# Sliding-window attention with a gated FFN: key tiles that repeat the last keys of the tile before, in batches 2 and 3

## The chip, the cores and the metric

The kernel runs on one core of a Trainium2 chip. The metric is the device time of one execution in microseconds (us); lower is better. Three runs of the kernel before took 254.18, 252.22 and 251.6 us, a median of 252.22 us.

A core has five engines with instruction queues of their own. TensorE (PE) multiplies matrices and loads the stationary operand of each product (PEld). VectorE (DVE), ScalarE (ACT) and GpSimd (POOL) work elementwise. SyncE (SP) only issues DMA transfers here. Each engine [...]waits on semaphores for what others produce. Sixteen DMA engines move the data.

## The reference

```python
# q, k, v: (4, 8, 768, 64) float32; n_sink = 4, window = 128
scores = (q @ k.transpose(0, 1, 3, 2)) / sqrt(64)
rel = pos[:, None] - pos[None, :]
keep = (pos[None, :] < 4) | ((rel >= 0) & (rel < 128))
a = softmax(where(keep, scores, -1e9))
x = (a @ v).transpose(0, 2, 1, 3).reshape(3072, 512)
out = (maximum(x @ w_gate, 0) * (x @ w_val)) @ w_out   # w_gate, w_val: 512 x 1536; w_out: 1536 x 512
```

Each query sees the four first keys (the sinks) and the 128 keys that end with itself. The output of attention goes, token by token, through a gated feed-forward network (FFN) with a ReLU on the gate.

## The kernel before

**Units.** A unit is a pair of heads of one batch: four units per batch, sixteen in all, so units 8 to 11 are batch 2 and units 12 to 15 batch 3. Its two heads lie on partitions 0 to 63 and 64 to 127 of `KQ`, which holds the transposed queries in its first 768 columns and the keys (`kE`) behind them, 768 columns in order and 408 more for "odd" key tiles. Four `KQ` buffers go round.

**Key tiles.** A key tile has 128 rows. Seven tiles cover the 768 keys. The even ones (0, 2, 4, 6) are plain slices of the keys; the odd ones (1, 3, 5) consist of the four sinks and 124 keys, and are copied together on GpSimd by `odd_tiles` and `sinks` (L185, L181). The table `SEG` lists, per group of tiles, which key tile is multiplied with which queries and where in the score tile it lands: groups 0, 1 and 2 have 3, 3 and 4 segments per head. In each group one segment of three columns serves the last three queries that a query tile still needs from a key tile two places back. `QSEG` says, per query tile, which key tiles it adds up: 16 matmuls per head. The values lie in `vn` by the same tiles, with a column of ones behind each head, so that the 65th output column is the sum of the weights.

**Steps of a unit.** `Sg(u, s)` computes the scores of one group for both heads on TensorE (L290), takes exp on ScalarE (L298) and multiplies by a 0/1 mask (`msk`) on VectorE (L300). `W(u)` multiplies these weights with the values on TensorE (L325, stationary operand `ee`, 65 columns) and divides by the sum on VectorE into `xn` (L331). In batches 0 and 1 TensorE transposes queries, keys and `xn`. In batches 2 and 3 DMA does: `load_rows` brings queries and keys (`qf`, `kf`), `cast_rows` makes them bf16 on GpSimd (`qn`, `kn`, L166), `to_dram` writes them to a scratch tensor, and `turn` reads them back transposed into `KQ` (L175). `x_to_dram` writes `xn` to the scratch tensor `xd` (L151) and `x_turn` reads it back transposed into `xT` (L155). `load_v` brings one value tile of all eight heads (L131) and `cast_v` casts it on GpSimd (L134). All these transfers are issued by SP.

**The order.** It is written out by hand. The FFN's first half is cut into 96 chunks, 24 per batch; the loop goes through these slots. A chunk (`chunk`) is eight matmuls of up to 396 columns (L362), a ReLU on ScalarE (L377) and a product on VectorE (L379). From slot 24 on each slot adds three matmuls of the FFN's second half (L404). The attention of the next batch is put between them by the table `plan`: batch 2's scores start in slot 29 and its `W`s stand in slots 35, 37, 39 and 41; batch 3's scores start in slot 48 and its `W`s stand in slots 56, 58, 61 and 63. Batch 2's chunks begin in slot 48. The table `prep` puts GpSimd's work and the transfers in front of a slot's chunk: batch 2's value loads in slots 23 to 29 and casts in 28 to 34, batch 3's loads in 44 to 50 and casts in 47 to 53. Two rows of it matter most:

```python
            prep[at["S", i, 0] - 1].append(("sinks", i))
            prep[at["W", i, 0] + 1].append(("xd", i))
            prep[at["W", i, 0] + 3].append(("xturn", i))
        for b, s0, s1 in ((2, 23, 28), (3, 44, 47)):
            for j in range(7):
                prep[s0 + j].append(("lv", b, j))
                prep[s1 + j].append(("v", b, j))
```

Within a slot the entries are issued in the order in which they were appended. In slots 33 and 34 GpSimd's list is therefore: the casts of unit 12's keys and queries, value tile 5 of batch 2, the odd key tiles of unit 10, value tile 6.

Each transfer from SP counts up one of eight semaphores in turn, and waits where needed for the transfer that used it before, eight places back.

Of the kernel before, what the change touches and what calls it, by code (L numbers as in the profile page):

```python
# [10 lines left out]
BF16 = mybir.dt.bfloat16  # L11
Alu = mybir.AluOpType
# [9 lines left out]
def kernel(  # L22
# [12 lines left out]
    nc = tc.nc  # L35
    B, H, S, D = q.shape
    assert (B, H, S, D) == (4, 8, 768, 64)
    NP = H // 2
# [7 lines left out]
    const = ctx.enter_context(tc.tile_pool(name="const", bufs=1))  # L46
# [4 lines left out]
    NQ, NE, NT = 3, 4, 4  # L51
# [5 lines left out]
    KQ = [const.tile([128, 2 * S + 408], BF16, name=f"KQ{i}") for i in range(NT)]  # L57
    qT = [x[:, 0:S] for x in KQ]
    kE = [x[:, S:2 * S + 408] for x in KQ]
# [8 lines left out]
    xT = [const.tile([128, NP, S], BF16, name=f"xT{i}") for i in range(2)]  # L68
# [2 lines left out]
    warm = const.tile([128, 2], F32, name="warm")  # L71
    idle = const.tile([128, 512], BF16, name="idle")
    msk = const.tile([128, 3, 512], BF16, name="msk")
    mb = const.tile([128, 2, 512], BF16, name="mb")
    band = const.tile([128, 256], BF16, name="band")

# [5 lines left out]
    ODD = S  # L82
# [11 lines left out]
    QSEG = [[(0, 0, 0)], [(0, 0, 128), (1, 0, 252)], [(1, 0, 376), (2, 1, 0), (0, 0, 504)],  # L94
            [(2, 1, 128), (3, 1, 252)], [(3, 1, 376), (4, 2, 0), (2, 1, 504)],
            [(4, 2, 128), (5, 2, 272)], [(5, 2, 396), (6, 2, 252), (4, 2, 416)]]

    PART = {0: (range(3), 0, CUT0), 1: (range(3, 7), CUT0, S), None: (range(7), 0, S)}

# [4 lines left out]
    U = [Unit(i) for i in range(B * NP)]  # L104
# [17 lines left out]
    VROW = [0, 116, 244, 368, 496, 620, 748]  # L122

    def load_v(b, j, r0=0, r1=128):
        r1 = min(r1, S - VROW[j])

        parts = [(0, 4, 0), (4, 16, VROW[j] + 4), (16, 128, VROW[j] + 16)] if j in (1, 3, 5) else [(0, 128, VROW[j])]
        for a0, a1, s0 in parts:
            a1 = min(a1, r1)
            if r0 <= a0 < a1:  # L130
                nc.sync.dma_start(out=vf[a0:a1, j, :, :], in_=v[b, :, s0:s0 + a1 - a0, :].rearrange("h s d -> s h d"))  # L131
# [10 lines left out]
    kqd = [nc.dram_tensor(f"kqd{i}", (2 * S, 128), BF16, kind="Internal").ap() for i in range(ND, B * NP)]  # L142


    xd = [nc.dram_tensor(f"xd{i}", (1008, 128), BF16, kind="Internal").ap() for i in range(ND, B * NP)]

    def x_to_dram(u):

        x, d = xn[u.i % 2], xd[u.i - ND]
        for t, r0, n, i in ((0, 0, 128, 4), (1, 128, 124, 3)):  # L150
            nc.sync.dma_start(out=d[r0:r0 + 252 * i, :].rearrange("(i r) c -> r i c", r=252)[0:n, :, :],  # L151
                              in_=x[0:n, t:t + 2 * i - 1:2, :])

    def x_turn(u):
        nc.sync.dma_start(out=xT[u.b % 2][:, u.p, :], in_=xd[u.i - ND][8:8 + S, :], transpose=True)  # L155
        for x in range(2):
            ready[u.b, u.p, x] = True

# [20 lines left out]
    def sinks(u, copy):  # L179
        e = kE[u.i % NT]  # L180
        copy(odd(e)[:, :, 0:4], e[:, 0:4].unsqueeze(1).to_broadcast([128, 3, 4]))  # L181

    def odd_tiles(u, copy):
        e = kE[u.i % NT]
        copy(odd(e)[:, :, 4:128], e[:, 120:876].rearrange("d (i c) -> d i c", c=252)[:, :, 0:124])  # L185
        sinks(u, copy)

    def load_w(m0, m1, which=(0, 1)):
        for w, dst in (((moe_w_gate, wg), (moe_w_val, wv))[x] for x in which):
# [37 lines left out]
    def setup2(g):  # L227
# [6 lines left out]
        if g == 2:  # L234
            cp(msk[:, 2, 252:272], band[:, 0:20])

    rot = [0]

    def pair():
# [38 lines left out]

    def Sg(u, s, ps=None):
        t, bias = u.i % NT, u.b == 0 and s in (0, 3)  # L280
        g, b0, n, segs = SEG[s]
        ps = ps or pair()
        at = [ps[h][:] if isinstance(ps, list) else ps[:, h, :] for h in range(2)]
        if bias:
            for h in range(2):
                nc.tensor.matmul(out=at[h][:, b0:n], lhsT=ident[:], rhs=mb[:, g, b0:n], start=True, stop=False,
                                 skip_group_check=True)
        for x0, q0, c0, c1 in segs:
            for h in range(2):
                nc.tensor.matmul(out=at[h][:, c0:c1], lhsT=kE[t][64 * h:64 * h + 64, x0:x0 + 128],  # L290
                                 rhs=qT[t][64 * h:64 * h + 64, q0:q0 + c1 - c0], start=not bias, stop=True,
                                 skip_group_check=True)
        x = ee[u.i % NE][:, g, :, b0:n]
        if isinstance(ps, list):
            for h in range(2):
                nc.scalar.activation(x[:, h, :], at[h][:, b0:n], Act.Exp, bias=0.0, scale=scale)
        else:
            nc.scalar.activation(x, ps[:, :, b0:n], Act.Exp, bias=0.0, scale=scale)  # L298
        if not bias:
            nc.vector.tensor_tensor(x, x, msk[:, g, b0:n].unsqueeze(1).to_broadcast([128, 2, n - b0]), op=Alu.mult)  # L300

    ready = {}

# [5 lines left out]

    def W(u, part=None, bank=None):  # L310

        tiles = PART[part][0]
        n, w = len(tiles), 65 * len(tiles)
        if bank is None:
            ps = pair()
            at = [ps[:, 0, 0:w], ps[:, 1, 0:w]]
            o = ps[:, :, 0:w].rearrange("p h (t e) -> p h t e", e=65)
        else:
            at = [bank[:, 0:w], bank[:, w:2 * w]]
            o = bank[:, 0:2 * w].rearrange("p (h t e) -> p h t e", h=2, e=65)  # L320
        for h in range(2):
            for t in tiles:
                c = 65 * (t - tiles[0])
                for i, (j, g, c0) in enumerate(QSEG[t]):
                    nc.tensor.matmul(out=at[h][:, c:c + 65], lhsT=ee[u.i % NE][:, g, h, c0:c0 + 128],  # L325
                                     rhs=vn[u.b % 2][:, j, 2 * u.p + h, 0:65],
                                     start=c == 0 and i == 0 and (bank is None or h == 0),
                                     stop=t == tiles[-1] and i == len(QSEG[t]) - 1, skip_group_check=True)
# [82 lines left out]
    with tc.manual_schedule():  # L411
# [91 lines left out]
        for i, ts in ((8, (17, 20, 21, 24)), (9, (18, 21, 22, 26)), (10, (20, 23, 24, 28)), (11, (22, 24, 26, 30)),  # L503
                      (12, (30, 33, 35, 38)), (13, (32, 35, 37, 40)), (14, (34, 37, 39, 43)), (15, (36, 39, 41, 45))):
            for t, what in zip(ts, ("rows", "castrows", "td", "turn")):
                prep[t].append((what, i))
            assert at["S", i - NP, 2] < ts[3] < at["S", i, 0] - 1, i
            prep[at["S", i, 0] - 1].append(("sinks", i))
            prep[at["W", i, 0] + 1].append(("xd", i))
            prep[at["W", i, 0] + 3].append(("xturn", i))  # L510

        for b, s0, s1 in ((2, 23, 28), (3, 44, 47)):
            for j in range(7):
# [5 lines left out]
        for s, (b, g, m) in enumerate(slots):  # L519
            for x in prep[s]:  # L520
                if x[0] == "kq":
                    cast_rows(U[x[1]])
                elif x[0] == "load":
                    load_rows(U[x[1]])
                elif x[0] == "half":
                    cast_half(x[1])
                elif x[0] == "w":
                    load_w(*x[1:])
                elif x[0] == "wo":
                    for c in range(3):  # L530
                        load_wo(c)
                elif x[0] == "rows":
                    if x[1] in (8, 9):
                        gate(U[x[1]])
                    load_rows(U[x[1]])
                elif x[0] == "castrows":
                    cast_rows(U[x[1]])
                elif x[0] == "td":
                    to_dram(U[x[1]])
                elif x[0] == "setup3":  # L540
                    setup3()
                elif x[0] == "xd":
# [72 lines left out]
```

## Time and profile before

| quantity | value |
|---|---|
| median of three runs | 252.22 us |
| the profiled execution | 252.45 us |
| its span in the trace | 250.4 us |
| TensorE busy | 238.6 us, 95% |
| VectorE, ScalarE busy | 116.6 and 120.6 us |
| GpSimd busy | 69.7 us, 28% |
| DMA packets | 75681, of them 53512 under 512 bytes; 40.07 MB |

The profile's page gives the busy time of each engine, then the span in 40 slices of 6.26 us, each digit a busy share in tenths, and then the chain of work that ended last: from the last instruction back to whatever released it, step by step. Groups of instructions follow, with line, engine, operation, tiles, shapes, count, busy time, the mean duration of one in ns, and the idle time ahead of them with what ended it. The busy time of overlapping matmuls is counted once, so their means are longer than their distance in time. In the timelines and in the chain each row has its start and its duration in us; "SPq" is SP's queue, whose rows are issues of transfers, and "DMA" in the chain is the time until one has landed.

### The profile page before, as it was taken

The page shows a single profiled execution, that of the slowest core. Times are in us where ns is not written, and L with a number is a line of the kernel's source. Part 1 is how long each engine was busy: PE and PEld are TensorE (multiplying, and loading weights), DVE is VectorE, ACT ScalarE, POOL GpSimd, SP SyncE. Part 2 cuts the span into 40 slices and gives each one's busy share as a digit, 9 for nine tenths or more (in the row PEclk, how much of TensorE's full clock was granted, in tenths as well). Part 3 has the DMA queues.
Part 4 walks back from the last instruction along what each step waited for, and adds up shares of the span by engine and source line. Part 5 has one row for each costly group of instructions (what it writes and reads, how often), then busy time and mean ns, then how long its engine had stood idle before and what let it go on. Part 6 is the DMA issues. An engine that isn't in the chain of part 4 may idle for free.

```text
span 250.4 us, 5321 instructions
## 1 busy us (share of the span) xinstructions
PE 238.6 (95%) x2084; PEld 139.9 (56%) x2084; DVE 116.6 (47%) x224; ACT 120.6 (48%) x220; POOL 69.7 (28%) x125
## 2 busy tenths in 40 slices
PE   7879969999999999999999999999999999999994
PEld 2456556655775555666555556565555555555443
DVE  5565854688662354687325546544322232222000
ACT  4849926999253455552336664532333323333111
POOL 7856664982633225631003600000000000000000
PEclk9999999999999999999999999999999999999999
DMA  6999999999989999899899311443211011110232
GB/s 207 251 211 259 245 338 235 213 164 219 337 274 231 242 184 323 278 230 210 211 227 229 82 42 39 106 106 77 75 44 42 0 42 46 43 42 1 86 126 84
DMA packets 75681, 40.07 MB, mean 160 GB/s; under 512 B 53512, under 2 KB 72712, under 8 KB 75656
## 3 DMA queue, kind: packets, MB, share of 16 engines
q1 hardware_dynamic: 67560, 34.10, 52.6%
q0 software_dynamic: 6864, 4.72, 12.7%
q10 hardware_dynamic: 1232, 0.92, 1.1%
q8 instruction: 16, 0.26, 0.4%
q14 instruction: 9, 0.07, 0.1%
HBM read 28.48 MB, written 11.25 MB: 159 GB/s over the span
## 4 chain that ended last, share of the span: by engine, by line
PE 70%; DMA 15%; SPq 6%; POOL 4%; issue 2%; ACT 1%; DVE 0%; POOLq 0%; DVEq 0%; ACTq 0%
PE g L362 38%; PE g L404 20%; SPq L131 5%; PE pp L325 4%; DMA vf<-in_v_dram 4%; DMA kf<-in_k_dram 4%; DMA wv<-in_moe_w_val_dram 3%; PE pp L404 3%; DMA qf<-in_q_dram 3%; PE pp L290 2%; POOL vn L134 1%; POOL ee L308 1%; SPq L113 1%; PE pp L398 1%; PE g L398 1%
## 5 line engine op out<-in xcount | busy, mean ns | idle before, releaser
L379 DVE TENSOR_TENSOR hT<-gs,g 128x384 bf16<-128x384 f32 (+2 forms) x96 | 53.0, 553 | 88.3 <-PE g L362 80.2
L377 ACT ACTIVATE gs<-g 128x384 f32<-128x384 f32 (+2 forms) x96 | 47.7, 497 | 77.0 <-PE g L362 75.9
L362 PE MATMUL g<-xT,wv 128*128 128x384 bf16 (+2 forms) x384 | 78.8, 326 | 2.7 <-DMA wv<-in_moe_w_val_dram 2.6
L362 PE MATMUL g<-xT,wg 128*128 128x384 bf16 (+2 forms) x384 | 78.8, 326 | 0.5 <-ACT xT L345 0.5
L404 PE MATMUL g<-wo,hT 128*128 128x512 bf16 x240 | 64.0, 379 | 0.3 <-ACT ot L408 0.2
L362 PEld LDWEIGHTS <-wv 128*128 128x128 bf16 x384 | 37.3, 98 | 29.1 <-DMA wv<-in_moe_w_val_dram 3.8
L362 PEld LDWEIGHTS <-wg 128*128 128x128 bf16 x384 | 36.2, 98 | 30.3
L298 ACT ACTIVATE ee<-pp 128x838 bf16<-128x838 f32 (+4 forms) x50 | 43.0, 904 | 9.5 <-PE pp L290 9.2
L404 PEld LDWEIGHTS <-hT 128*128 128x128 bf16 x276 | 25.5, 98 | 23.8 <-issue 0.7
L300 DVE TENSOR_TENSOR ee<-ee,msk 128x838 bf16<-128x838 bf16 (+3 forms) x44 | 32.2, 738 | 13.8 <-ACT ee L298 13.2
L134 POOL CAST vn<-vf 128x512 bf16<-128x512 f32 x27 | 18.6, 706 | 33.7 <-DMA vf<-in_v_dram 33.7
L325 PEld LDWEIGHTS <-ee 128*128 128x128 bf16 x512 | 18.1, 97 | 5.1 <-issue 3.2
L408 ACT COPY ot<-g 128x512 f32<-128x512 f32 x20 | 11.7, 587 | 17.5 <-PE g L404 17.5
L325 PE MATMUL pp<-vn,ee 128*128 128x65 bf16 x488 | 18.2, 193 | 1.4 <-POOL vn L134 1.3
L331 DVE TENSOR_TENSOR xn<-pp,rn 128x896 bf16<-128x896 f32 (+2 forms) x18 | 17.0, 943 | 0.6
L290 PEld LDWEIGHTS <-KQ 64*128 64x128 bf16 x328 | 10.9, 94 | 10.1 <-issue 8.2
L290 PE MATMUL pp<-KQ 64*128 64x3 bf16 (+5 forms) x316 | 15.8, 221 | 0.0
L166 POOL CAST kn<-kf 128x768 bf16<-128x768 f32 x12 | 10.2, 851 | 17.2 <-DMA kf<-in_k_dram 8.9
L166 POOL CAST qn<-qf 128x768 bf16<-128x768 f32 x12 | 11.3, 940 | 2.8 <-DMA qf<-in_q_dram 2.5
L185 POOL COPY KQ<-KQ 128x372 bf16<-128x372 bf16 x12 | 6.3, 529 | 11.5 <-DMA KQ<-kqd 6.8
L345 ACT COPY xT<-g 128x372 bf16<-128x372 bf16 (+2 forms) x10 | 5.4, 545 | 6.8 <-PE g L342 6.8
L404 PE MATMUL pp<-wo,hT 128*128 128x512 bf16 x36 | 8.1, 379 | 0.0
(80 smaller groups left out, 105.5 us busy)
## 6 DMA issues: line engine op xcount, KB each, us to landing
out_dram<-ot SPq DMA_DIRECT2D x23, 256.0 KB
kf<-in_k_dram SPq DMA_DIRECT2D x12, 384.0 KB
qf<-in_q_dram SPq DMA_DIRECT2D x12, 384.0 KB
vf<-in_v_dram SPq DMA_DIRECT2D x12, 256.0 KB
vf<-in_v_dram SPq DMA_DIRECT2D x12, 224.0 KB
kf<-in_k_dram SPq DMA_DIRECT2D x8, 192.0 KB
wo<-in_moe_w_out_dram POOLq DMA_DIRECT2D x3, 512.0 KB, 8.6
kqd<-qn SPq DMA_DIRECT2D x8, 192.0 KB
```

The costliest lines, as they stand in the source:

```text
L131: nc.sync.dma_start(out=vf[a0:a1, j, :, :], in_=v[b, :, s0:s0 + a1 - a0, :].rearrange("h s d -> s h d"))
L134: copy(vn[b % 2][0:rows, j, :, 0:64], vf[0:rows, j, :, :])
L166: nc.gpsimd.tensor_copy(dst[u.i % 2][:].rearrange("p (n h d) -> p h n d", n=NR, h=2), src[u.i % NQ][:].rearrange("p (h n d) -> p h n d", n ...
L290: nc.tensor.matmul(out=at[h][:, c0:c1], lhsT=kE[t][64 * h:64 * h + 64, x0:x0 + 128], rhs=qT[t][64 * h:64 * h + 64, q0:q0 + c1 - c0], start ...
L298: nc.scalar.activation(x, ps[:, :, b0:n], Act.Exp, bias=0.0, scale=scale)
L300: nc.vector.tensor_tensor(x, x, msk[:, g, b0:n].unsqueeze(1).to_broadcast([128, 2, n - b0]), op=Alu.mult)
L325: nc.tensor.matmul(out=at[h][:, c:c + 65], lhsT=ee[u.i % NE][:, g, h, c0:c0 + 128], rhs=vn[u.b % 2][:, j, 2 * u.p + h, 0:65], start=c == 0 ...
L331: nc.vector.tensor_tensor(x.rearrange("p t (h d) -> p h t d", h=2), o[:, :, :, 0:64], r.unsqueeze(3).to_broadcast([128, 2, n, 64]), op=Alu ...
L362: nc.tensor.matmul(out=ps[:, 0:n], lhsT=w[:, ko, m * 128:(m + 1) * 128], rhs=x[:, ko, c], start=ko == 0, stop=ko == KO - 1)
L377: nc.scalar.activation(gs[:, 0:n], gp[:, 0:n], Act.Relu, bias=0.0, scale=1.0)
L379: nc.vector.tensor_tensor(h[:, m, c], gs[:, 0:n], vp[:, 0:n], op=Alu.mult)
L404: nc.tensor.matmul(out=op, lhsT=hT[b % 2][:, m, t * 128:(t + 1) * 128], rhs=wo[:, m, :], start=m == 0, stop=m == FM - 1)
```

## The change

In batches 2 and 3 the key tiles are cut anew, at keys 0, 128, 256, 380, 504, 625, 746 and 768 (`K2`). From tile 2 on a tile begins with repeated rows (`LEAD`): the four sinks (tiles 2, 4, 6), and the last 3 or 6 keys ahead of the tile before it (tiles 3 and 4, tiles 5 and 6). A query tile then needs its own key tile and the one before it, and nothing else. Groups 0, 1 and 2 have 2, 2 and 3 segments per head (`SEG2`), `QSEG2` has 13 matmuls per head, and a second mask (`msk2`) is built by `setup4` on GpSimd in slots 25 to 27. `key_tiles` takes the place of `odd_tiles` and puts tiles 2 to 6 together behind the keys in `KQ`, which grows by 232 columns. `load_v` loads each value tile in the same order of rows, in up to four transfers, and `x_to_dram` stores the seven query tiles without overlap in four transfers. Batches 0 and 1 stay as they are.

```diff
+    K2 = [0, 128, 256, 380, 504, 625, 746, S]
+    LEAD = [(0, 0), (0, 0), (4, 0), (0, 3), (4, 3), (0, 6), (4, 6)]
+    PLACE = [0, 128] + [ODD + 128 * i for i in range(5)]
+    SEG2, QSEG2, at2 = {}, [[] for _ in range(7)], 0
+    for t in range(7):
+        if t % 2 == 0 and t < 6:
+            at2 = 0
+            SEG2[t // 2] = (t // 2, 0, 0, [])
+        g2 = min(t // 2, 2)
+        w = K2[min(t + 2, 7)] - K2[t]
+        SEG2[g2] = (g2, 0, at2 + w, SEG2[g2][3] + [(PLACE[t], K2[t], at2, at2 + w)])
+        QSEG2[t].append((t, g2, at2))
+        if t < 6:
+            QSEG2[t + 1].append((t, g2, at2 + K2[t + 1] - K2[t]))
+        at2 += w
...
     def load_v(b, j, r0=0, r1=128):
-        r1 = min(r1, S - VROW[j])
-
-        parts = [(0, 4, 0), (4, 16, VROW[j] + 4), (16, 128, VROW[j] + 16)] if j in (1, 3, 5) else [(0, 128, VROW[j])]
+        if b >= 2:
+            s, d = LEAD[j]
+            x, end = K2[j] - s - d, s + d + K2[j + 1] - K2[j]
+            parts = [(0, s, 0), (s, s + d, K2[j - 1] - d)] * (s + d > 0)
+            parts += [(s + d, 16, K2[j]), (16, end, x + 16)] if s + d else [(0, end, K2[j])]
+            parts = [x for x in parts if x[0] < x[1]]
+        else:
+            parts = [(0, 4, 0), (4, 16, VROW[j] + 4), (16, 128, VROW[j] + 16)] if j in (1, 3, 5) else [(0, 128, VROW[j])]
+            r1 = min(r1, S - VROW[j])
...
-        for t, r0, n, i in ((0, 0, 128, 4), (1, 128, 124, 3)):
-            nc.sync.dma_start(out=d[r0:r0 + 252 * i, :].rearrange("(i r) c -> r i c", r=252)[0:n, :, :],
-                              in_=x[0:n, t:t + 2 * i - 1:2, :])
+        for t in range(0, 7, 2):
+            n, i = K2[t + 1] - K2[t], min(2, 7 - t)
+            nc.sync.dma_start(out=d[K2[t]:K2[t] + i * n, :].rearrange("(i r) c -> r i c", r=n), in_=x[0:n, t:t + i, :])
...
-        nc.sync.dma_start(out=xT[u.b % 2][:, u.p, :], in_=xd[u.i - ND][8:8 + S, :], transpose=True)
+        nc.sync.dma_start(out=xT[u.b % 2][:, u.p, :], in_=xd[u.i - ND], transpose=True)
...
+    def key_tiles(u, copy):
+        e = kE[u.i % NT]
+        copy(e[:, ODD:].rearrange("d (i c) -> d i c", c=128)[:, 0:5:2, 0:4], e[:, 0:4].unsqueeze(1).to_broadcast([128, 3, 4]))
+        for t in range(2, 7):
+            s, d = LEAD[t]
+            for c, k0, n in ((s + d, K2[t], K2[t + 1] - K2[t]), (s, K2[t - 1] - d, d)):
+                if n:
+                    copy(e[:, PLACE[t] + c:PLACE[t] + c + n], e[:, k0:k0 + n])
...
+    def setup4(g):
+        cp, ms = nc.gpsimd.tensor_copy, nc.gpsimd.memset
+        for t, (_, _, c0, c1) in zip(range(2 * g, 7), SEG2[g][3]):
+            s, d = LEAD[t]
+            cp(msk2[:, g, c0:c1], band[:, s + d:s + d + c1 - c0])
+            if t in (3, 5):
+                nc.gpsimd.affine_select(out=msk2[:, g, c0:c1], in_=msk2[:, g, c0:c1], compare_op=Alu.is_ge, fill=0.0,
+                                        base=126, pattern=[[0, c1 - c0]], channel_multiplier=-1)
+            if s + d:
+                x = msk2[0:s + d, g, c0:c1]
+                ms(x, 1.0)
+                nc.gpsimd.affine_select(out=x, in_=x, compare_op=Alu.is_ge, fill=0.0, base=-s,
+                                        pattern=[[-1, c1 - c0]], channel_multiplier=1)
+            if s:
+                ms(msk2[0:s, g, c0:c1], 1.0)
+        if g == 0:
+            ms(msk2[0:4, 0, 0:256], 1.0)
+            for i in range(NT):
+                ms(kE[i][:, ODD + 511:ODD + 640], 0.0)
+        if g == 2:
+            for i in range(NE):
+                ms(ee[i][:, 2, :, 404:514], 1.0)
...
+        for g2 in range(3):
+            prep[25 + g2].append(("setup4", g2))
...
-                    odd_tiles(U[x[1]], nc.gpsimd.tensor_copy)
+                    key_tiles(U[x[1]], nc.gpsimd.tensor_copy)
```

`Sg` and `W` take `SEG2`, `msk2` and `QSEG2` where the unit's batch is 2 or 3.

More of the change, by code (lines that the diff above doesn't have):

```diff
@@ L55 @@
     vn = [const.tile([128, 7, H, 66], BF16, name=f"vn{i}") for i in range(2)]
-    KQ = [const.tile([128, 2 * S + 408], BF16, name=f"KQ{i}") for i in range(NT)]
+    KQ = [const.tile([128, 2 * S + 640], BF16, name=f"KQ{i}") for i in range(NT)]
     qT = [x[:, 0:S] for x in KQ]
-    kE = [x[:, S:2 * S + 408] for x in KQ]
+    kE = [x[:, S:2 * S + 640] for x in KQ]
     ee = [const.tile([128, 3, 2, 640], BF16, name=f"ee{i}") for i in range(NE)]
@@ L73 @@
     msk = const.tile([128, 3, 512], BF16, name="msk")
+    msk2 = const.tile([128, 3, 512], BF16, name="msk2")
     mb = const.tile([128, 2, 512], BF16, name="mb")
@@ L142 @@
     kqd = [nc.dram_tensor(f"kqd{i}", (2 * S, 128), BF16, kind="Internal").ap() for i in range(ND, B * NP)]
-    xd = [nc.dram_tensor(f"xd{i}", (1008, 128), BF16, kind="Internal").ap() for i in range(ND, B * NP)]
+    xd = [nc.dram_tensor(f"xd{i}", (S, 128), BF16, kind="Internal").ap() for i in range(ND, B * NP)]
     def x_to_dram(u):
         x, d = xn[u.i % 2], xd[u.i - ND]
-        for t, r0, n, i in ((0, 0, 128, 4), (1, 128, 124, 3)):
-            nc.sync.dma_start(out=d[r0:r0 + 252 * i, :].rearrange("(i r) c -> r i c", r=252)[0:n, :, :],
-                              in_=x[0:n, t:t + 2 * i - 1:2, :])
+        for t in range(0, 7, 2):
+            n, i = K2[t + 1] - K2[t], min(2, 7 - t)
+            nc.sync.dma_start(out=d[K2[t]:K2[t] + i * n, :].rearrange("(i r) c -> r i c", r=n), in_=x[0:n, t:t + i, :])
     def x_turn(u):
-        nc.sync.dma_start(out=xT[u.b % 2][:, u.p, :], in_=xd[u.i - ND][8:8 + S, :], transpose=True)
+        nc.sync.dma_start(out=xT[u.b % 2][:, u.p, :], in_=xd[u.i - ND], transpose=True)
         for x in range(2):
@@ L280, in Sg @@
         t, bias = u.i % NT, u.b == 0 and s in (0, 3)
-        g, b0, n, segs = SEG[s]
+        g, b0, n, segs = (SEG if u.b < 2 else SEG2)[s]
+        mask = msk if u.b < 2 else msk2
         ps = ps or pair()
@@ L299, in Sg @@
         if not bias:
-            nc.vector.tensor_tensor(x, x, msk[:, g, b0:n].unsqueeze(1).to_broadcast([128, 2, n - b0]), op=Alu.mult)
+            nc.vector.tensor_tensor(x, x, mask[:, g, b0:n].unsqueeze(1).to_broadcast([128, 2, n - b0]), op=Alu.mult)
     ready = {}
@@ L310, in W @@
     def W(u, part=None, bank=None):
-        tiles = PART[part][0]
+        tiles, seg = PART[part][0], QSEG if u.b < 2 else QSEG2
         n, w = len(tiles), 65 * len(tiles)
@@ L323, in W @@
                 c = 65 * (t - tiles[0])
-                for i, (j, g, c0) in enumerate(QSEG[t]):
+                for i, (j, g, c0) in enumerate(seg[t]):
                     nc.tensor.matmul(out=at[h][:, c:c + 65], lhsT=ee[u.i % NE][:, g, h, c0:c0 + 128],
@@ L327, in W @@
                                      start=c == 0 and i == 0 and (bank is None or h == 0),
-                                     stop=t == tiles[-1] and i == len(QSEG[t]) - 1, skip_group_check=True)
+                                     stop=t == tiles[-1] and i == len(seg[t]) - 1, skip_group_check=True)
         x, r = xn[u.i % 2][:, tiles[0]:tiles[0] + n, :], rn[u.i % 2][:, :, 0:n]
@@ L548 @@
                 elif x[0] == "sinks":
-                    odd_tiles(U[x[1]], nc.gpsimd.tensor_copy)
+                    key_tiles(U[x[1]], nc.gpsimd.tensor_copy)
+                elif x[0] == "setup4":
+                    setup4(x[1])
                 elif x[0] == "lv":
```

## The prediction

> **What bounds the kernel now.** I read the page first.
>
> ```profile
> PE 238.6 (95%) x2084; PEld 139.9 (56%) x2084; DVE 116.6 (47%) x224; ACT 120.6 (48%) x220; POOL 69.7 (28%) x125
> ...
> PE   7879969999999999999999999999999999999994
> ...
> DMA  6999999999989999899899311443211011110232
> ...
> PE 70%; DMA 15%; SPq 6%; POOL 4%; issue 2%; ACT 1%; DVE 0%; POOLq 0%; DVEq 0%; ACTq 0%
> ```
>
> TensorE is busy 95% of 250.4 us, so a matmul less is time saved. But until about 135 us the DMA engines are full too, and 21% of the chain that ended last is DMA and SP's queue. Where it leaves TensorE counts for this change, so I followed it through batch 2's attention (84 to 103 us):
>
> ```profile
> 91.88 0.42 SPq L175
> ...
> 92.34 4.38 DMA kf<-in_k_dram
> ...
> 96.85 0.95 POOL kn L166
> ...
> 98.66 0.61 POOL vn L134
> 99.27 0.18 POOL KQ L185
> ...
> 99.66 0.19 POOL KQ L181
> 99.85 0.57 POOL vn L134
> ...
> 100.46 0.70 PE pp L325 x18
> ```
>
> The first `W` of batch 2 (unit 8) stops for its last value tile. That cast stands on GpSimd behind unit 10's key copies, the fifth value cast and unit 12's `kn`/`qn` casts, which wait for unit 12's keys. SP issues those keys late, as its timeline shows:
>
> ```profile
> 84.67 4.10 SPq L175 DMA_TRANSPOSE KQ<-kqd  x1
> 88.81 1.76 SPq L131 DMA_DIRECT2D vf<-in_v_dram  x4
> 90.68 1.62 SPq L175 DMA_TRANSPOSE KQ<-kqd  x1
> 92.34 0.58 SPq L161 DMA_DIRECT2D kf<-in_k_dram  x1
> ```
>
> SP runs without a gap. From the landing (96.73, by the trace's semaphore events, as all landings here) to TensorE (100.46) it is 3.73 us. So whatever lengthens SP's list, the transfers before unit 12's keys, or GpSimd's list here reaches TensorE in full.
>
> **What the Trainium skill says.** (1) "DMA: Bandwidth & Descriptors", section "Why a DMA increments its semaphore by 16 and not by 1": a transfer issued from SP runs on k engines, the largest number up to 16 that divides the slowest dimension, the lowest-numbered k; the sequencer posts the other 16-k increments at once. The trace agrees: its semaphore events show 16 updates for transfers of 128 and 112 rows, but 13 for 12 rows, 11 for 20, and 5 for 4 and for 124, that is k engines and one early update. That they are the lowest-numbered, and so the same ones each time, no view here shows. (2) "TensorE: Matmul & The Clock Gate", section "Back-to-back issue gap": up to 64 columns a matmul costs an issue floor of about 25 ns. The trace: 30 ns at 65 columns, about 23 for a pair of 3-column ones (below). (3) "Perfetto Trace Analysis", section "DMA Instruction — HWDGE (DVE, Sync)": the profiled bar is the issue alone, not the data movement. Here unit 12's keys take 0.58 us to issue and 4.38 to land.
>
> **TensorE: what goes.** Per unit of batches 2 and 3, score segments fall from 10 to 7 per head (three of 3 columns go) and value matmuls from 16 to 13.
>
> ```profile
> L325 PE MATMUL pp<-vn,ee 128*128 128x65 bf16 x488 | 18.2, 193 | 1.4 <-POOL vn L134 1.3
> L290 PE MATMUL pp<-KQ 64*128 64x3 bf16 x92 | 7.7, 163 | 0.0
> ```
>
> Means overlap, so I price by steps. 32 value matmuls take 0.96 us in the chain: 30 ns each, 6 fewer, 0.18 us. The two heads of a segment run side by side; 6 pairs of 1006 columns take 0.56 us, 7 pairs of 918 take 0.54. At 2.4 columns per ns that leaves 0.14 and 0.16 us: 23 ns a pair. Three pairs are 0.07, and 17 columns less (1425 to 1408) 0.01. Together 0.26 us a unit, 2.1 us for eight. This lies on the path. ScalarE's and VectorE's tiles shrink by 1% (0.01 us each); both idle half the time, which hides it either way.
>
> **GpSimd: what comes.** Once, `setup4`: 7 copies, 7 affine selects, 17 memsets, queued after unit 11's casts (end 76.6 us). Start to start, a copy of 372 elements takes 0.44 us and one of 12 takes 0.14, so 0.13 + 0.83 ns per element; a memset of 266 takes 0.27 and of 442 0.40; an affine select of 256 takes 0.47 with its wait. That gives 2.2 + 2.9 + 4.4 = 9.5 us (8 to 11), to 86.1. Only 1.5 us of idle time covers it (unit 8's copies began at 78.04). Per unit, ten copies replace two: 1.75 us for 0.58 to 0.63 (2.4 if small ones do not overlap). Unit 8's scores of segment 1 need the first four (0.75 us): 86.9, against TensorE at 85.5, a stall of 1.3 us. Segment 0 reads tiles 0 and 1 in place and waits for none. The wait is new for tiles 3, 5 and 6 one by one: behind it on TensorE stand three second-FFN matmuls and the next chunk, and ScalarE's exp and VectorE's mask wait for the scores (the mask also for `setup4`, done by then). This stall is later swallowed by the larger one at `W`. Unit 10's copies stand between kn and the last value cast: +1.1 us there.
>
> **SP's queue and the DMA engines: what comes.** Value loads grow from 13 to 19 issues per batch, x stores from 2 to 4 per unit; an issue takes about 0.38 us. Tile 4 gains three issues, which fall into the wait inside the 4.10 us transpose (the smallest takes 1.62). Tile 6 gains three, uncovered: 1.2 us before unit 12's keys. The rows stored fall from 884 to 768: 116 packets, 0.1 us a unit at the packet price below, taken as nothing because SP's issues, not the data, are late there. The x transpose reads from row 0 instead of 8, the same 768 rows; with no reason for a loss, I take nothing here as well (0.1 either way).
>
> The largest item is a shape. Tiles 3 and 5 now end in loads of 111 rows, not 112. 111 = 3 x 37, so by (1) they run on 3 engines: 888 packets of 256 B are 296 an engine, not 56. A packet's price, from a saturated microsecond (133 to 134):
>
> ```profile
> DMA packets 1129, 0.28 MB, mean 285 GB/s; under 512 B 1129, under 2 KB 1129, under 8 KB 1129
> ```
>
> 1129 / 16 = 71 an engine, 14 ns each. 240 extra packets are 3.4 us (2.9 to 4.6 for 12 to 19 ns) on these three, and every later transfer needs them. Two such loads, 6.8 us, precede unit 12's keys. Gaps in which these engines idled take some back: by the DMA share of each microsecond, some 2.5 us lay idle between 83 and 93, and an engine that ran early had more. The keys land between 99.4 and 101.9, middle 100.6, for 96.73. `W` resumes 3.73 + 1.1 later, 105.4; less 0.1 for matmuls gone within it, TensorE is **4.9 us late**. `setup4`'s stall and SP's 1.2 us lie inside this.
>
> To slot 48 three more `W`s and six score groups return 0.7: 4.2 late. There xT of unit 11 is due. SP stays with `W`, and its 8 extra x-store issues (3.2 us) are taken back but for 0.8 us by its waits inside transposes; xT lands at 129.16 for a need at 130.7 before, 1.5 of slack, so it loses its slack and costs about 0.3. After two units' scores TensorE is 4.3 late. In batch 3 both 111-row loads recur, before the casts:
>
> ```profile
> 139.76 0.62 POOL L134 CAST vn<-vf 128x512 bf16<-128x512 f32 x1 [0.32 <-DMA vf<-in_v_dram]
> 140.32 0.50 POOL L185 COPY KQ<-KQ 128x372 bf16<-128x372 bf16 x1
> ```
>
> The first is value tile 5, and unit 14's copies queue behind it; before, segment 1 needed them at 145.6. Tile 3's load (landed 137.4 before) lands 5.7 (4.9 and the 0.8 of SP's queue) plus 3.4 later, about 146; tile 4 takes 0.9, tile 5 4.2: 151.2. Cast and four copies bring 152.5, TensorE is there at 149.9: **2.6 us stall** (0 to 6). 6.9 late, less 0.9 for what `W` and scores still save: +6.0.
>
> 252.45 us (span 250.4 plus 2.0 around it) + 6.0 = **258.5 us**. The runs' median is 252.22, 0.2 lower, within their scatter (251.6 to 254.18), so I keep 258.5.
>
> **Rivals.** (A) is the forecast, 255 to 262.
> (B) The 111-row loads do not hold anything up: they spread over more engines, or idle time absorbs them. Then keys come 1.2 late by SP, GpSimd adds 1.1: 2.3 late at `W`, minus 1.9 still to be saved: +0.4, 252.9 us (to 254.8). For: DMA load falls in gaps. Against: 124-row stores demonstrably use 4 engines.
> (C) Not slower: GpSimd's and SP's additions are hidden and only TensorE's 2.1 us remain, 250.3 us. It decides at `W`: 0.2 of the 2.1 is saved before it and swallowed, so TensorE must resume by 102.3. GpSimd's copies take 1.1 of these 1.9 us, so unit 12's keys must land by 97.5, 0.8 later than now: no loss at all to the 111-row loads and only two thirds of SP's 1.2. Against it: SP's gapless rows above.
> (D) The stalls multiply: each transfer waits for the eighth before it, so SP stops behind a 111-row load, and x transposes come later than slot 48 allows (3 us) while batch 3 loses 5: about 263 to 266.
> The change does what its words say: its instruction lists show 48 score and 48 value matmuls fewer.
>
> **How the numbers follow.** A 0.60, D 0.13, B 0.20, C 0.07. 1% (2.5 us) is about what a measurement of this kernel can tell from no change. Slower by over 1%: A, D and the top of B, 0.80. Within: 0.18. Faster by over 1%: 0.02, as 2.1 us is the ceiling. The range 253.3 to 263.5 takes in the middle of B and the lower end of D.
>
> **What would show it.** At unit 8's `W`, TensorE's wait for a value cast grows from 0.92 to over 4 us, and the chain before it goes through unit 12's keys landing near 100; 4 semaphore updates for the 111-row loads; GpSimd busy about 19 us more (9.5 + 8 x 1.2); a wait of TensorE on GpSimd near 150 us. It is wrong if keys land below 98 us, if `setup4` takes over 14 us (then the stall at unit 8's scores rules), or if the stall in batch 3 is absent.

## The result, and the profile after

The changed kernel took 265.75 us (median of four runs, 264.5 to 268.27) against 252.9 for the kernel before in the same comparison: a ratio of 1.052, 95% interval 1.042 to 1.062. The forecast was 258.5 us with a range up to 263.5, so the direction held and the size did not. The profiled execution took 265.61 us with a span of 263.9 us, 13.5 us longer than before's 250.4. The forecast had +6.0.

The page of the changed kernel, in the order in which before's was read, with the row of TensorE's granted clock added:

```profile
PE 242.6 (92%) x1988; PEld 138.9 (53%) x1988; DVE 116.0 (44%) x224; ACT 120.8 (46%) x220; POOL 86.8 (33%) x220
...
PE   7879889999999992799999959999999999999994
...
PEclk9999999999999999599999986999999999999999
DMA  7999999999998639779887321136301111100232
...
PE 65%; DMA 15%; SPq 7%; POOL 6%; issue 2%; ACT 2%; DVE 1%; ACTq 0%; POOLq 0%; DVEq 0%
...
L389 PE MATMUL pp<-vn,ee 128*128 128x65 bf16 x440 | 17.1, 195 | 7.6 <-POOL vn L161 7.6
...
L354 PE MATMUL pp<-KQ 64*128 64x3 bf16 (+11 forms) x268 | 16.5, 236 | 4.1 <-POOL KQ L222 4.0
```

96 matmuls are gone, as forecast, 48 of them value matmuls (488 to 440), yet TensorE is busy 4.0 us longer. The row of slices shows two holes (digits 2 and 5, near 104 and 155 us), and behind each of them the clock row drops from 9 to 5 or 6. Before had neither. The last two rows say what TensorE waited for: 7.6 us for a value cast instead of 1.3, and 4.0 us for GpSimd's key copies, for which before's page shows no wait. GpSimd is busy 17 us more.

SP's timeline ahead of unit 12's keys, to be held against the same stretch of before:

```profile
82.40 1.05 SPq L158 DMA_DIRECT2D vf<-in_v_dram  x3
83.55 3.88 SPq L473 DMA_DIRECT2D out_dram<-ot  x1
87.48 1.38 SPq L158 DMA_DIRECT2D vf<-in_v_dram  x4
88.96 1.82 SPq L202 DMA_TRANSPOSE KQ<-kqd  x1
90.83 6.18 SPq L158 DMA_DIRECT2D vf<-in_v_dram  x7
97.11 1.34 SPq L202 DMA_TRANSPOSE KQ<-kqd  x1
98.49 0.59 SPq L188 DMA_DIRECT2D kf<-in_k_dram  x1
```

A 111-row load is the last of the three at 82.40 (issued 83.15, landed 89.29); the very next issue, a store of output rows, takes 3.88 us instead of some 0.4. The same happens inside the row of 6.18 us: the second such load goes out at 91.69 and lands at 97.83, and the issue behind it, a load of 4 rows, takes 3.78 us. Unit 12's keys are therefore issued 6.15 us later than before. Meanwhile the DMA engines are mostly idle, as the stretches of 2 us show (the last two columns are the DMA engines' mean busy share and GB/s):

```profile
82.00:84.00 2.00, 2.00 (x13) 1.13 (x12) 0.55 (x1) 0.49 (x1) 1.67 (x7) 1.00 1.12 325
84.00:86.00 2.00, 1.38 (x11) 0.52 (x9) 0.56 (x1) 1.07 (x2) 1.81 (x11) 1.00 0.24 56
86.00:88.00 2.00, 1.70 (x11) 0.85 (x12) 0.76 (x1) 1.43 (x2) 2.00 (x10) 1.00 0.26 61
...
94.00:96.00 2.00, 2.00 (x20) 1.12 (x19) 0.73 (x2) 0.75 (x2) 0.00 (x0) 1.00 0.24 55
```

A quarter of the engine time is used. In before the three stretches have shares of 0.84, 1.21 and 0.89. The load's semaphore shows 4 updates, which is three engines and one early update, as the prediction read it from the Trainium skill ("DMA: Bandwidth & Descriptors", section "Why a DMA increments its semaphore by 16 and not by 1").

The chain from the keys to TensorE:

```profile
98.49 4.16 DMA kf<-in_k_dram
...
102.70 0.83 POOL kn L193
...
104.44 0.61 POOL vn L161
...
105.19 1.56 POOL KQ L222 x9
106.75 0.56 POOL vn L161
...
107.36 0.93 PE pp L389 x14
```

It is the chain of before, step for step, 6.9 us later: `W` resumes at 107.36 instead of 100.46. TensorE's own timeline shows the two waits there, and what follows:

```profile
105.11 0.27 PE L389 MATMUL pp<-vn,ee 128*128 128x65 bf16 x2 [4.93 <-POOL vn L161]
107.36 0.93 PE L389 MATMUL pp<-vn,ee 128*128 128x65 bf16 x14 [1.98 <-POOL vn L161]
...
108.75 1.46 PE L468 MATMUL g<-wo,hT 128*128 128x512 bf16 x3
110.01 1.48 PE L426 MATMUL g<-xT,wg 128*128 128x384 bf16 x4
...
113.47 0.81 PE L426 MATMUL g<-xT,wg 128*128 128x384 bf16 x4
...
157.01 0.75 PE L354 MATMUL pp<-KQ 64*128 64x248 bf16 x4 [3.20 <-POOL KQ L222]
157.69 1.46 PE L468 MATMUL g<-wo,hT 128*128 128x512 bf16 x3
158.94 1.49 PE L426 MATMUL g<-xT,wg 128*128 128x384 bf16 x4
160.22 1.49 PE L426 MATMUL g<-xT,wv 128*128 128x384 bf16 x4
```

A row of four chunk matmuls takes 1.48 us instead of 0.81 right after each hole, and three of the second FFN half 1.46 instead of 0.81. By 113 and 164 us they are back. That is TensorE at half clock, and no step of the prediction had it. What it costs can be read off. From the resumption of unit 8's `W` to the start of unit 9's `W` it is 7.41 us here; the same stretch takes 5.34 in the kernel with 112-row loads below (103.39 to 108.73): 2.1 us. From 157.01 to unit 12's `W` at 164.22 it is 7.21 us; these matmuls' rows at full clock add up to some 4.3 (six groups of 0.65, and 0.33 for the scores): 2.9 us. Together 5.0 us. The trace's granted clock gives the same loss another way: it is 0.50 from 105.0 to 111.8 us and from 156.2 to 163.0 us, and 1.00 around them. TensorE works 4.5 and 6.0 us within these stretches after its waits, and half of that is 2.2 and 3.0 us.

The chain in batch 3 has the cause of the second hole:

```profile
143.25 4.31 SPq L158
...
149.78 4.14 SPq L158
...
154.66 1.90 DMA vf<-in_v_dram
```

Two more 111-row loads, each holding SP's next issue for over 4 us. The second is value tile 5's and lands at 155.83; GpSimd casts the tile then, and unit 14's key copies stand behind that cast, as its own timeline shows:

```profile
155.98 0.61 POOL L161 CAST vn<-vf 128x512 bf16<-128x512 f32 x1 [3.81 <-DMA vf<-in_v_dram]
...
156.66 1.62 POOL L222 COPY KQ<-KQ 128x124 bf16<-128x124 bf16 x9
```

The last row of the chain is a load of tile 6, which lands at 156.56 while the cast of tile 5 runs; the copies do not need it.

The sum, as TensorE's lateness against before: 6.9 at unit 8's `W`, plus 2.1 of half clock, less 0.7 for matmuls gone, gives 8.3 at slot 48 (its first chunk row starts at 138.27 against 130.08: 8.2). Plus 3.2 of waiting and 2.9 of half clock in batch 3, less 1.1 for the matmuls gone from there on, it would be 13.2; 13.5 is measured, so 0.3 us is not accounted for.

### The profile page after: what moved, and what is told of

Its sections match the earlier page's. It is cut to its first block, busy times and chain, and to the rows that moved or that the text cites. A ratio compares the mean times of both kernels' runs of the same rounds, so it can differ in the third digit from the quotient of the medians.

```text
span 263.9 us, 5265 instructions
## 1 busy us (share of the span) xinstructions
PE 242.6 (92%) x1988; PEld 138.9 (53%) x1988; DVE 116.0 (44%) x224; ACT 120.8 (46%) x220; POOL 86.8 (33%) x220
## 4 chain that ended last, share of the span: by engine, by line
PE 65%; DMA 15%; SPq 7%; POOL 6%; issue 2%; ACT 2%; DVE 1%; ACTq 0%; POOLq 0%; DVEq 0%
PE g L426 35%; PE g L468 18%; DMA qf<-in_q_dram 6%; SPq L158 6%; DMA vf<-in_v_dram 6%; DMA kf<-in_k_dram 4%; PE pp L389 3%; PE pp L354 3%; PE pp L468 3%; ACT ee L362 1%; POOL KQ L222 1%; POOL vn L161 1%; POOL msk L278 1%; POOL qn L193 1%; POOL msk L287 1%
## 5 line engine op out<-in xcount | busy, mean ns | idle before, releaser
L426 PE MATMUL g<-xT,wg 128*128 128x384 bf16 (+2 forms) x384 | 80.3, 331 | 0.7 <-ACT xT L409 0.5
L468 PE MATMUL g<-wo,hT 128*128 128x512 bf16 x240 | 66.0, 389 | 0.0
L362 ACT ACTIVATE ee<-pp 128x838 bf16<-128x838 f32 (+7 forms) x50 | 43.0, 900 | 19.2 <-PE pp L354 18.3
L364 DVE TENSOR_TENSOR ee<-ee,msk 128x838 bf16<-128x838 bf16 (+6 forms) x44 | 31.3, 715 | 17.3 <-ACT ee L362 15.2
L389 PE MATMUL pp<-vn,ee 128*128 128x65 bf16 x440 | 17.1, 195 | 7.6 <-POOL vn L161 7.6
L389 PEld LDWEIGHTS <-ee 128*128 128x128 bf16 x464 | 17.0, 98 | 10.7 <-issue 8.8
L354 PE MATMUL pp<-KQ 64*128 64x3 bf16 (+11 forms) x268 | 16.5, 236 | 4.1 <-POOL KQ L222 4.0
L354 PEld LDWEIGHTS <-KQ 64*128 64x128 bf16 x280 | 9.7, 94 | 15.1 <-issue 7.6
L222 POOL COPY KQ<-KQ 128x124 bf16<-128x124 bf16 (+4 forms) x72 | 14.3, 251 | 0.0
L394 DVE RECIPROCAL rn<-pp 128x14 f32<-128x14 f32 (+2 forms) x18 | 4.2, 231 | 11.5 <-PE pp L389 11.2
```

The lines of the kernel that those rows point to most:

```text
L222: copy(e[:, PLACE[t] + c:PLACE[t] + c + n], e[:, k0:k0 + n])
L364: nc.vector.tensor_tensor(x, x, mask[:, g, b0:n].unsqueeze(1).to_broadcast([128, 2, n - b0]), op=Alu.mult)
L426: nc.tensor.matmul(out=ps[:, 0:n], lhsT=w[:, ko, m * 128:(m + 1) * 128], rhs=x[:, ko, c], start=ko == 0, stop=ko == KO - 1)
L468: nc.tensor.matmul(out=op, lhsT=hT[b % 2][:, m, t * 128:(t + 1) * 128], rhs=wo[:, m, :], start=m == 0, stop=m == FM - 1)
```

## The experiments

Two questions had to be told apart: is it the 111-row loads and not GpSimd's or SP's other additions; and is the half clock a time of its own, or does something else bind there anyway. The kernel before has its own run beside every group.

### 112 rows instead of 111

```diff
-            x, end = K2[j] - s - d, s + d + K2[j + 1] - K2[j]
+            x, end = K2[j] - s - d, 128 if j in (3, 5) else s + d + K2[j + 1] - K2[j]
```

Value tiles 3 and 5 take one more row, which the mask gives no weight.

> The changed kernel, with value tiles 3 and 5 of batches 2 and 3 loaded to row 127: one more key row, whose weight the mask makes zero, so the last load of each has 112 rows. Theory (the 111-row loads run on 3 engines and cost everything beyond TensorE's 2.1 us): unit 12's keys land near 97.9 us of the span, the first W of batch 2 waits about 2 us in all for value casts, the wait near 150 us and both stretches of halved clock vanish, 253 us (251.5 to 255). Rival 1 (the list of SP with its 20 more issues, whatever their rows): little changes, 263 or more. Rival 2 (GpSimd's setup4 and ten copies): 261 or more, as they are untouched.

252.95 us, ratio 1.001 (0.998 to 1.004). The whole loss is in this one row: its removal takes 12.8 us away, with `setup4`, the ten key copies, the extra value loads and the extra stores all still there. Unit 12's keys land at 97.58, and TensorE's timeline has three short waits left:

```profile
87.81 0.28 PE L354 MATMUL pp<-KQ 64*128 64x248 bf16 x2 [1.27 <-POOL KQ L222]
88.64 0.28 PE L354 MATMUL pp<-KQ 64*128 64x245 bf16 x2 [0.54 <-POOL KQ L222]
103.39 0.58 PE L389 MATMUL pp<-vn,ee 128*128 128x65 bf16 x14 [1.09 <-POOL vn L161]
```

They take 2.9 us where before has one wait of 0.92: that is where the 2.1 us of saved matmuls go. This is rival B of the prediction: 252.95 us for 252.9, or 0.24 us more than the kernel before in the same comparison for a forecast of 0.4.

### The kernel before, with loads of 111 rows, and of 96

```diff
+        if b >= 2 and j in (3, 5):
+            parts = parts[:2] + [(16, 127, VROW[j] + 16), (127, 128, VROW[j] + 127)]
```

The second kernel has 112 in place of 127 there: the same four extra transfers, cut as 96 and 16 rows.

> The kernel before, with the last load of value tiles 3 and 5 in batches 2 and 3 cut after 111 rows: 111 + 1 rows in place of 112, the same data, nothing else of the change. Theory: the 111-row loads land 6 us after their issue, SP's next issue is held about 4 us, the first W of batch 2 stops 5 us or more, the clock halves after it, batch 3's scores stop too: 263 us (259 to 267). Rivals 1 and 2: four more small issues are all that is new, at most 2 us: 253 to 255.

> Control of the one before: the same loads cut after 96 rows (96 + 16), both of which divide by 16, so the count of issues and the data are the same as with 111 + 1. Theory: within 1 us of the kernel before, 253 to 254. Rival 1 (a further issue is what costs): as the cut at 111, above 258.

111 and 1 rows: 264.62 us, ratio 1.040 (1.029 to 1.051). 96 and 16 rows: 253.87 us, ratio 1.003 (0.999 to 1.006). Four more transfers cost 0.6% at most by the interval, and perhaps nothing; the shape makes before nearly as slow as the changed kernel, by the same way. TensorE in the first of the two:

```profile
104.92 0.27 PE L327 MATMUL pp<-vn,ee 128*128 128x65 bf16 x2 [4.51 <-POOL vn L136]
106.05 1.15 PE L327 MATMUL pp<-vn,ee 128*128 128x65 bf16 x18 [0.87 <-POOL vn L136]
...
108.92 1.48 PE L364 MATMUL g<-xT,wg 128*128 128x384 bf16 x4
...
155.55 0.73 PE L292 MATMUL pp<-KQ 64*128 64x252 bf16 x10 [1.89 <-POOL KQ L183]
...
157.47 1.49 PE L364 MATMUL g<-xT,wg 128*128 128x384 bf16 x4
```

The wait and the half clock are both there, in batch 3 too, where a wait of only 1.89 us is enough: the granted clock is 0.50 from 155.7 to 159.1 us. In its list of transfers the issue right behind each 111-row load takes 3.84 and 3.60 us. Unit 12's keys land at 101.88, 3.9 us later than with 96 and 16 rows (97.95).

### Keeping TensorE busy while it waits

```diff
+        if (u.i, s) == (14, 1):
+            spin(13, gvn[0] % 3)
...
+                    if (u.i, h, t, i) in ((8, 0, 5, 1), (8, 0, 6, 1)):
+                        spin({5: 21, 6: 8}[t], gvn[0] % 3)
```

The changed kernel, with products of a zero tile whose result nothing reads put where TensorE waits at unit 8's `W` (21 and 8 of them) and at unit 14's segment 1 (13).

> The changed kernel, with products of a zero tile put on TensorE into its stops: 21 and 8 of 512 columns (0.22 us each) before the two value matmuls of unit 8's W that wait, 13 before the scores of unit 14's segment 1. Theory (each stop leaves TensorE at half clock for 3 us and more afterwards, 5.4 us of the 13.5 in all): the granted clock stays 1.00 throughout and the time falls by 4 to 5.5 us, to 260.5 to 261.5. Rival (the slow matmuls come from something else, such as transfers at the same time): no gain, 265 to 267, or slower where the products outlast a stop.

261.95 us, ratio 1.038 (1.033 to 1.044): 3.8 us less than the changed kernel, and a little less than the 4 to 5.5 us that I expected. The slowest of its executions took 262.86 us, the fastest of the changed kernel 264.5. TensorE fills the same time with work of no use, and what follows runs at full clock:

```profile
107.07 0.58 PE L393 MATMUL pp<-vn,ee 128*128 128x65 bf16 x14 [0.30 <-POOL vn L161]
...
108.56 0.81 PE L430 MATMUL g<-xT,wg 128*128 128x384 bf16 x4
...
137.80 0.32 PE L430 MATMUL g<-xT,wg 128*128 128x384 bf16 x1 [1.23 <-DMA xT<-xd]
```

Chunk matmuls take 0.81 at once, not 1.48, and the granted clock is 1.00 from 24 us to the end of the work. A new wait for xT at slot 48 takes 1.2 us of the gain back; 5.0 less 1.2 is 3.8, the gain of the medians. So the half clock is time of its own, and idleness is what brings it.

### 112 rows in batch 2 only

```diff
+            x, end = K2[j] - s - d, 128 if b == 2 and j in (3, 5) else s + d + K2[j + 1] - K2[j]
```

> The change with 112-row loads in batch 2 only; batch 3 keeps its loads of 111 rows. Theory (two separate stalls, each with a half clock behind it): batch 2 as with 112 rows everywhere, then a wait of 2.5 to 3.5 us at unit 14's scores of segment 1 and about 3 us of half clock, 257 to 259.5. Rival 1 (batch 3's stall exists only because batch 2 made everything late): under 254.5. Rival 2 (one stall would do all the harm): over 262.

257.27 us, ratio 1.019 (1.011 to 1.026). The two stalls are separate.

```profile
103.19 0.58 PE L389 MATMUL pp<-vn,ee 128*128 128x65 bf16 x14 [1.39 <-POOL vn L161]
150.31 0.75 PE L354 MATMUL pp<-KQ 64*128 64x248 bf16 x4 [2.72 <-POOL KQ L222]
...
152.25 1.48 PE L426 MATMUL g<-xT,wg 128*128 128x384 bf16 x4
153.53 0.87 PE L426 MATMUL g<-xT,wv 128*128 128x384 bf16 x4
```

Batch 2 looks as with 112 rows everywhere. Batch 3 waits 2.72 us, and from there to unit 12's `W` (156.18) it is 5.87 us for some 4.3 at full clock: 1.6 us of half clock, where I had expected about 3. 252.95 + 2.72 + 1.6 = 257.3. Of the 12.8 us that 111 rows cost, 4.3 are batch 3's when nothing else is late.

### The 111-row loads from ScalarE's queue

```diff
-                nc.sync.dma_start(out=vf[a0:a1, j, :, :], ...
+                (nc.scalar if (a1 - a0) % 16 == 15 and b >= 2 and a0 == 16 else nc.sync).dma_start(out=vf[a0:a1, j, :, :], ...
```

> The change, its four loads of 111 rows issued from ScalarE's queue instead of SP's; all else as it is. Theory (SP itself stood still for about 4 us behind each such load, and that put unit 12's keys late): SP issues unit 12's keys before 94.5 us instead of 98.5, they land at 97 to 99.5, TensorE's wait at unit 8's value product is under 3.5 us, and the time is 253.5 to 257.5. Rival (the three DMA engines are what is late, SP's stop is only how it shows): keys land after 101, 261 or more.

265.17 us, ratio 1.046 (1.039 to 1.054): my theory fell, the rival held. I had thought that SP's stop behind its own load was the cause and that the three engines alone would leave the keys nearly in time. The two loads go out at 77.76 and 81.64, 5 and 10 us ahead of their places in SP's list (83.15 and 91.69), and still unit 12's keys are issued at 100.54 and land at 104.32, later than in the changed kernel. SP stops as well, though the loads are not in its queue:

```profile
78.40 2.55 SPq L158 DMA_DIRECT2D vf<-in_v_dram  x4
81.06 5.73 SPq L202 DMA_TRANSPOSE KQ<-kqd  x1
...
90.17 4.70 SPq L158 DMA_DIRECT2D vf<-in_v_dram  x4
```

The row of 5.73 us is a single issue. The row of 4.70 us is not: its four issues take some 0.3 us each, and between them SP waits for the transfers eight places back, a transposed read (landed at 92.59, next issue at 92.60) and the second 111-row load itself (landed at 94.22, next issue at 94.24).

The transfers around the loads land late too: the two loads take 8.6 and 12.6 us from issue to landing, and a load of 128 rows that SP issues at 78.40 needs 7.9. Its semaphore updates in the trace show why. Of the 16, 13 have come by 82.44, and three come at 85.94 to 86.28, when the three engines of the first 111-row load report as well (85.77 to 86.39). So the backlog of three engines holds up what runs on all sixteen, whichever queue the load comes from. As the loads also went out earlier and shared the eight semaphores with SP's transfers, this run does not price the change of queue alone. What in the transposed read waits for the three engines, and what held SP's next issue in the changed kernel, no view shows, and I leave both open.

### The order before, with the last casts first

```diff
-                prep[s1 + j].append(("v", b, j))
+                if b == 2 and j > 4:
+                    prep[33].insert(j - 5, ("v", b, j))
+                else:
+                    prep[s1 + j].append(("v", b, j))
```

The kernel before, with value tiles 5 and 6 of batch 2 cast ahead of unit 12's keys.

> The kernel before, with batch 2's value tiles 5 and 6 cast ahead of unit 12's keys. Theory (the 0.92 us wait at unit 8's value product is real time on the path): 251.4 to 252.2, 0.994 to 0.998 of before. Rival (xT of unit 11 at slot 48 takes it back): within 0.3 us of before.

251.55 us, ratio 0.997 (0.994 to 0.999), about 0.9 us, the length of the wait at unit 8's `W`, which is gone from its trace. That wait was on the path, and an order of casts was enough to lose it.

### 112 rows, with GpSimd's list rearranged

```diff
-        for g2 in range(3):
-            prep[25 + g2].append(("setup4", g2))
+        prep[11].append(("setup4", 0))
+        prep[14] += [("setup4", 1), ("setup4", 2)]
+        prep[27].append(("setup4", 3))
```

This on top of the 112 rows and of the order of casts just shown; `setup4(3)`, split off from `setup4(2)`, is the memset of `ee`, which has to stay behind batch 1.

> The change with 112-row loads as before, and GpSimd's list rearranged: the new masks are built in earlier idle time (slots 11 and 14), and batch 2's value tiles 5 and 6 are cast ahead of unit 12's keys instead of behind them. With 112-row loads alone the kernel waited 1.8 us at unit 8's scores and 1.1 at its value product. Theory (the saved matmuls are worth 2.1 us wherever no wait takes them back, and the wait of 0.9 at the value product goes too): 249.3 to 251.2 us, 0.985 to 0.994 of before. Rival (what is saved is taken back at the next wait, xT of unit 11 at slot 48 or batch 3's values): 252 to 253.5.

250.29 us, ratio 0.990 (0.985 to 0.995). All three waits in batch 2 are gone, and one has come:

```profile
128.73 0.32 PE L426 MATMUL g<-xT,wg 128*128 128x384 bf16 x1 [1.42 <-DMA xT<-xd]
```

It is the wait at slot 48 that the prediction priced at 0.3 us. With TensorE in time, SP's list with its eight extra stores brings xT of unit 11 at 128.69, late by 1.4 us. So the next kernel issues one transposed read, of unit 14's queries and keys, a slot later, behind that xT:

```diff
-                      ... (14, (34, 37, 39, 43)) ...
+                      ... (14, (34, 37, 39, 44)) ...
```

> The rearranged kernel with 112-row loads, and unit 14's transposed read of queries and keys issued one slot later, behind xT of unit 11 instead of ahead of it. In the rearranged kernel TensorE waited 1.42 us at slot 48 for that xT, and the transposed read ahead of it on SP took 1.37 us. Theory (the last of the saved matmuls' 2.1 us sits in this wait): 248.7 to 249.9 us, 0.983 to 0.989 of before, no wait at slot 48. Rival (xT comes no earlier, as the transfer ahead of both is what holds them): 250 to 250.8.

248.8 us, ratio 0.987 (0.983 to 0.991).

```profile
127.84 0.32 PE L426 MATMUL g<-xT,wg 128*128 128x384 bf16 x1 [0.56 <-DMA xT<-xd]
```

The wait shrinks to 0.56 us; I had expected none to be left, but xT lands 0.9 us earlier, not the 1.4 that the read ahead of it had taken on SP. This version beats both kernels, though its step over the one before it (0.987 for 0.990) lies within the intervals. Of its 1.3%, about 0.3% is the order of casts, which before could have had too; the remaining 1.0% is 2.5 us, with intervals of over 1 us, beside the 2.1 us that the saved matmuls were priced at.

## Why the prediction was wrong

The direction, the place and the cause were right. Two terms of the sum were not: the half clock behind a stall was put at nothing, and the slack in SP's list was spent twice. Lateness of TensorE, forecast and measured:

| step | forecast, us | measured, us |
|---|---|---|
| `setup4`, stall at unit 8's scores (swallowed) | 9.5, 1.3 | 9.1, 0.84 |
| unit 12's keys land | 100.6 | 102.65 |
| from there until `W` resumes | 4.8 | 4.7 |
| late at unit 8's `W` | 4.9 | 6.9 |
| half clock behind it | not in the sum | 2.1 |
| returned up to slot 48 | -0.7 | -0.8 |
| wait at slot 48 | 0.3 | 0 |
| stall in batch 3 | 2.6 | 3.2 |
| half clock behind it | not in the sum | 2.9 |
| returned from slot 48 on | -1.1 | -0.8 (what is left) |
| sum | 6.0 | 13.5 |

**The half clock, 5.0 of the missing 7.5 us.** The prediction priced a stall at its length. TensorE's longest wait in before, once its first slots are over, is 0.92 us (1.67 with them), and its clock row is 9 throughout, so the trace at hand did not have the price; but I had forecast waits of 5 and 2.6 us and did not ask what the engine does after them. The Trainium skill says it ("TensorE: Matmul & The Clock Gate", section "What's actually happening"): the clock goes to half after about 3.4 us without work, in windows that run freely, and comes back after about as long a stretch of work. With that page an estimate of some 1.7 us (half of 3.4) would have stood in the sum, for the first stall alone, as a wait of 2.6 us is shorter than the page's window.

The traces agree with the page's window and not with its wait. Wherever the half clock comes inside a run it lasts 3.41 us or two or three times as long: 6.83 us after both stalls here, 3.41 with 112 rows in batch 2 only, 10.24 with the loads on ScalarE's queue. But shorter waits brought it too: 3.20 and 2.72 us, and 1.89 in the kernel before with 111-row loads. No wait of 1.89 us or more left the clock alone. Below that the length does not decide. Waits of 1.67 us (before, at 31 us), of 1.39 (112 rows in batch 2), and of 1.32 and 0.54 close together (batch 3 with the loads on ScalarE's queue) did nothing; 1.28, 0.50 and 0.34 us within 3.4 us of each other (112 rows in batch 2, at 31 to 35 us) brought 3.41 us of half clock. Where a wait falls in the windows may be what decides, but no run varies that.

**"Some 2.5 us lay idle" and "`setup4`'s stall and SP's 1.2 us lie inside this": 2.0 us.** The price of the load was about right: 240 more packets were priced at 3.4 us, and the issues behind the two loads took 3.88 and 3.78 us in place of some 0.5. What failed is that the slack was spent twice. From value tile 3 to unit 12's keys SP's list is longer than before's by 6.7 us of this holding and by 2.0 us for six more issues (tiles 4 and 6). It is shorter by 2.6 us, because the transposed reads take 1.82 and 1.34 us instead of 4.10 and 1.62. That leaves 6.1 us, and the keys land 0.2 sooner after their issue: 5.9. What came back is about the 2.5 us that I had seen idle, but I had let the same time cover the loads and the added issues. For the loads alone the forecast's middle value, keys 3.9 us later, is what 111 rows in the kernel before show (101.88 against 97.95); for the added issues alone it is 0.85 us (97.58 with 112 rows, 96.73 before). While SP stood still and three engines worked, nothing was issued in which the others could get ahead: the stretches at 0.24 of the engines' time above. In where the keys land, executions of the same list also scatter: 102.65 here and 101.74 in the kernel with zero products.

**Batch 3: 3.2 for 2.6 us.** Right in mechanism and inside the stated 0 to 6; without batch 2's stall it was 2.72. That the size came so near is partly luck: tile 5 landed at 155.8 for a forecast of 151.2 and TensorE came at 153.8 for 149.9, both some 4 us later. By its own terms the forecast's "about 146" for tile 3 is also 146.5 (137.4 + 5.7 + 3.4), which would make its stall 3.0.

**Slot 48.** No wait, as TensorE came 8.2 us late itself. From the start of unit 11's `W` to the landing of its xT it is 12.5 us in the changed kernel and 12.4 in before, so the eight extra stores were indeed taken back. Where TensorE comes early they are not: in the rearranged kernel the same stretch takes 15.1 us (113.55 to 128.69), and TensorE waits 1.42.

**GpSimd's and TensorE's terms** held: `setup4` took 9.1 us, ten key copies 1.7 (105.05 to 106.75 in the chain), and a value matmul 30 ns (26 of them take 0.78 us to the next row, 32 took 0.96).

**The rivals.** B (252.9) is what the kernel does with 112 rows. C, only TensorE's gain, needed a rearranged list as well. D gave 263 to 266 and so the right number, but not by its mechanism: the held issue is the very next one, not the eighth after it (that wait shows only with the loads on ScalarE's queue), xT was not late for slot 48, and what multiplied the stalls was the clock.

## What to carry to other kernels

Look at the number of rows in every transfer that a retiling makes: 111 rows instead of 112 cost 12.8 us here, while four transfers more cost 0.6% at most, and one row of padding was the whole repair. Only loads on three engines were tried; what five or eight would cost, no run shows.

Spend the slack of a queue once: the 2.6 us that SP's waits gave back could cover the loads or the added issues, not both. Price a TensorE wait with the half clock behind it: every wait of 1.89 us and more had it here, at 1.5 to 3 us of time where the loss was read off. And where many small savings are spread over a kernel, follow each to the next wait: they are only worth something once that wait has been moved.

## What the runs showed that I had not expected

- TensorE's clock halved after waits of 1.89, 2.72, 3.20 us and more and stayed full after one of 1.39. The half clock lasted 3.41 us or two or three times that. Products of a zero tile in the wait kept the clock up and saved 3.8 us net.
- A load of 111 rows x 8 heads of 256 bytes from SP lands 5.8 to 6.6 us after its issue, and the next issue of SP is held for 3.5 to 4.3 us, while the engines together move some 56 GB/s. Two such loads issued 3.9 us apart from ScalarE's queue took 8.6 and 12.6 us, and three of the 16 engines of SP's own loads came late with them.
